# One software DMA queue shared by weight loads, gathers and result scatters: a new order, one more early weight and six output buffers

## Chip, core and metric

One core of one Trainium2 chip runs the whole program. Times are device microseconds. Each profile is of one of the executions whose times are listed. Chips differ (the kernel before had medians from 239.5 to 250.9 us in the five sets of rounds) and one core has slow executions too, so every comparison below is between kernels run on the same chip in the same rounds, or between stretches inside profiles. The record marks slow executions as such.

## The reference, cut to what matters

```
attn = masked_attention(q, k, v)          # 4 batches, 8 heads, 768 tokens, 64 dims
x    = attn as [3072 tokens, 512]
for e in range(8):                        # each token belongs to one of 8 experts
    out[tokens of e] = relu(x[tokens of e] @ w1[e]) @ w2[e]
# w1[e] is 512x1024, w2[e] is 1024x512, float32 in HBM
```

## The kernel before

Attention writes its result to a DRAM scratch tensor. Tokens are then gathered by expert, transposed, sent through two layers and scattered to their rows of the output. Three sorts of DMA are issued by GpSimd and share one software queue (q0 of the profile: 7936 packets, 26.75 MB): weight loads (float32 in HBM, cast to float16 on the way, 1 MiB landed), gathers of 128 token rows, and scatters of 128 result rows.

```
def load_w(e, which):                     # 16 of these, 4 buffers for each layer
    nc.gpsimd.dma_start(out=<fp16 tile>, in_=<fp32 weights in HBM>)

def load_xe(pr, g):                       # 28 gathers: 7 per pair of experts
    nc.gpsimd.indirect_dma_start(out=xe_of(pr, g), in_=x_d, in_offset=map_i[...])

def finish_group(pr, g, ps):              # 28 scatters: 7 per pair
    o = opool.tile(...)                   # one of 4 output buffers
    nc.vector.tensor_copy(out=o, in_=ps)  # the sums of TensorE's matmuls, 0.69 us
    nc.gpsimd.indirect_dma_start(out=out, out_offset=out_i[...], in_=o)

for pr in range(E // 2):                  # the late part of the expert stage
    layer2(a); layer2_half(pr); layer2(b_)        # 3 + 1 + 3 groups
    <weights for later experts>; <drain>; <gathers>
    for g in range(NG): x_transpose(pr + 2, g)    # TensorE, then a VectorE copy
    layer1(a + 4, 0, CAP); layer1(b_ + 4, 0, CAP)
# ... attention, early experts, routing and a fallback loop cut
```

The output copy and the copies of the transposes are both on VectorE, in program order. An output copy that waits for a buffer therefore holds back everything behind it (in the changed kernel the copy at 181.16 us had waited 6.10 us, and the transposes' copies followed at 181.76).

The softmax here doesn't subtract the row's maximum and nothing guards it: scores larger than these inputs give would overflow.

## Time and profile before

| | before |
|---|---|
| runs (the profile is of the second) | 239.22, 241.62, 238.91 us |
| span of the profile | 239.7 us |
| TensorE busy | 82% |
| start of expert 0's second layer to last matmul | 134.84 to 234.01, so 99.2 us |
| of it, TensorE standing still at two places | 12.09 and 3.48 us |

The fifth row is the one the change is about. The profile lines that show it stand in the prediction. In a timeline the columns are start, duration, engine, line, operation, operands, count, and in brackets the idle time before it with what ended it. The granted clock is the share of its full clock that TensorE was given, by the profile, and "halved" means 0.5 (in the kernel before from 149.1 to 162.7 us).

### The profile page before, as it was taken

The page shows a single profiled execution, that of the slowest core. Times are in us where ns is not written, and L with a number is a line of the kernel's source. Part 1 is how long each engine was busy: PE and PEld are TensorE (multiplying, and loading weights), DVE is VectorE, ACT ScalarE, POOL GpSimd, SP SyncE. Part 2 cuts the span into 40 slices and gives each one's busy share as a digit, 9 for nine tenths or more (in the row PEclk, how much of TensorE's full clock was granted, in tenths as well). Part 3 has the DMA queues.
Part 4 walks back from the last instruction along what each step waited for, and adds up shares of the span by engine and source line. Part 5 has one row for each costly group of instructions (what it writes and reads, how often), then busy time and mean ns, then how long its engine had stood idle before and what let it go on. Part 6 is the DMA issues. An engine that isn't in the chain of part 4 may idle for free. (4 is left out here: it accounts for less than half of the span.)

```text
span 239.7 us, 4769 instructions
## 1 busy us (share of the span) xinstructions
PE 197.7 (82%) x1935; PEld 123.7 (52%) x1935; DVE 107.8 (45%) x251; ACT 93.7 (39%) x117; POOL 110.3 (46%) x143
## 2 busy tenths in 40 slices
PE   0489999699998999988988992067999479999990
PEld 0235666456664666588988741035654145544440
DVE  1337899999968767642022130034003160033431
ACT  2177678548862787424655400001640005600000
POOL 0546675358153514743875460038611580036552
PEclk9999999999997999999999999559999999999998
DMA  6999999999999530699899899926999549913332
GB/s 209 300 314 288 307 288 244 299 340 291 242 320 328 128 131 26 122 280 243 163 198 263 151 215 214 252 108 122 213 215 228 210 178 176 182 45 133 136 117 89
DMA packets 42909, 49.79 MB, mean 208 GB/s; under 512 B 27263, under 2 KB 35712, under 8 KB 42882
## 3 DMA queue, kind: packets, MB, share of 16 engines
q0 software_dynamic: 7936, 26.75, 48.5%
q1 hardware_dynamic: 34368, 22.02, 32.9%
q10 hardware_dynamic: 578, 0.66, 1.1%
q8 instruction: 17, 0.28, 0.4%
q14 instruction: 10, 0.08, 0.1%
HBM read 56.76 MB, written 10.49 MB: 280 GB/s over the span
## 5 line engine op out<-in xcount | busy, mean ns | idle before, releaser
L333 ACT ACTIVATE eT<-sp 128x1024 f16<-128x1024 f32 (+2 forms) x68 | 60.3, 916 | 35.5 <-PE sp L311 34.7
L708 ACT ACTIVATE hT<-h 128x512 f16<-128x512 f32 (+2 forms) x48 | 32.1, 669 | 77.6 <-PE h L701 77.6
L732 PE MATMUL o<-w,hT 128*128 128x512 f16 x192 | 44.6, 389 | 15.6 <-DVE oute L714 15.6
L701 PE MATMUL h<-xT,w 128*128 128x256 f16 (+2 forms) x384 | 50.4, 290 | 1.6 <-DVE xT L686 1.6
L716 POOL DMA_INDIRECT out_dram<-oute,out_i x28 | 27.8, 994 | 51.6 <-DVE oute L714 30.1
L714 DVE COPY oute<-o 128x512 f32<-128x512 f32 x24 | 16.5, 692 | 74.9 <-PE o L732 54.6
L701 PEld LDWEIGHTS <-w 128*128 128x128 f16 x384 | 38.9, 114 | 12.1 <-DVE xT L686 1.7
L732 PEld LDWEIGHTS <-hT 128*128 128x128 f16 x192 | 18.7, 99 | 39.9 <-issue 19.5
L660 POOL DMA_INDIRECT xe<-x_tok,map_i x24 | 24.5, 1019 | 25.2 <-DVE xe L801 7.8
L387 PE MATMUL av<-ve,eT 128*128 128x65 f16 (+3 forms) x532 | 31.3, 196 | 4.9 <-DVE xb L400 2.8
L387 PEld LDWEIGHTS <-eT 128*128 128x128 f16 (+3 forms) x572 | 25.6, 99 | 15.3 <-issue 7.9
L311 PE MATMUL sp<-qT,kT 64*128 64x192 f16 (+6 forms) x244 | 26.0, 277 | 1.9 <-DVE kT L281 1.6
L311 PE MATMUL sp<-c16s 128*128 128x128 f16 (+1 forms) x132 | 25.9, 278 | 0.5 <-ACT eT L333 0.3
L155 POOL CAST q<-q 128x768 f16<-128x768 f32 x15 | 13.0, 869 | 23.6 <-PE tpq L276 11.8
L155 POOL CAST k<-k 128x768 f16<-128x768 f32 x16 | 13.2, 827 | 16.8 <-DMA k<-in_k_dram 15.8
L281 DVE COPY qT<-tpq 128x768 f16<-128x768 f16 x16 | 15.2, 950 | 8.2 <-PE tpq L276 8.2
L683 DVE COPY xT<-xtp 128x512 f16<-128x512 f16 x24 | 9.1, 418 | 21.1 <-PE xtp L676 20.4
L400 DVE TENSOR_TENSOR xb<-av,rcp 128x384 f16<-128x384 f32 x32 | 17.8, 557 | 1.1
L311 PEld LDWEIGHTS <-kT 64*128 64x128 f16 x244 | 9.7, 95 | 16.4 <-issue 7.1
L281 DVE COPY kT<-tpk 128x768 f16<-128x768 f16 x16 | 15.2, 948 | 3.2 <-PE tpk L276 3.2
L176 POOL CAST ve<-v 128x384 f16<-128x384 f32 x32 | 15.8, 524 | 0.8 <-DMA v<-in_v_dram 0.8
L276 PE MATMUL tpq<-c16s,q 128*128 128x128 f16 x96 | 9.4, 237 | 6.4 <-DVE q L155 5.4
(80 smaller groups left out, 130.2 us busy)
## 6 DMA issues: line engine op xcount, KB each, us to landing
w<-in_moe_w_dram POOLq DMA_DIRECT2D x16, 1024.0 KB, 11.6
q<-in_q_dram SPq DMA_DIRECT2D x16, 384.0 KB, 6.1
k<-in_k_dram SPq DMA_DIRECT2D x16, 384.0 KB, 6.1
v<-in_v_dram SPq DMA_DIRECT2D x32, 192.0 KB, 5.7
x_tok<-xb SPq DMA_DIRECT2D x4, 768.0 KB, 6.9
out_dram<-oute,out_i POOLq DMA_INDIRECT x28, 2.8
xe<-x_tok,map_i POOLq DMA_INDIRECT x24, 7.5
c16s<-c ACTq DMA_DIRECT2D x1, 336.5 KB, 4.6
```

The costliest lines, as they stand in the source:

```text
L155: eng.tensor_copy(out=t[:].rearrange("p t h d -> p h t d"), in_=q32_t[nm, n][:])
L281: nc.vector.tensor_copy(out=d[:], in_=cell["ps"][:].rearrange("d t p -> d p t"))
L311: nc.tensor.matmul(out=sp[:, c : c + w], lhsT=lhsT, rhs=rhs, start=bank not in begun, stop=True, skip_group_check=True,)
L333: nc.scalar.activation(out=eT[n, r // 3][:, r % 3, c0:c1], in_=sp[:, c0:c1], func=AF.Exp, scale=scale)
L387: nc.tensor.matmul(out=ps[m0:m1, it, :], lhsT=eT[n, r // 3][kk, r % 3, c : c + w], rhs=rhs, start=(x == 0), stop=(x == len(mms) - 1), skip ...
L400: nc.vector.tensor_tensor(out=xb[b][:, :, h * D : (h + 1) * D], in0=ps[:, :, 0:D], in1=rcp[:].unsqueeze(2).to_broadcast([P, NSO, D]), op=A ...
L660: nc.gpsimd.indirect_dma_start(out=xe_of(pr, g), out_offset=None, in_=x_d[0 : 1 + nb * S, :], in_offset=bass.IndirectOffsetOnAxis(ap=map_i ...
L701: nc.tensor.matmul(out=pv[:, a, c0:c1], lhsT=w_t[e, 1][:, c // 2, c % 2, fc * 512 + fr : (fc + 1) * 512 : 4], rhs=xT_t[e][:, c, c0:c1], st ...
L708: nc.scalar.activation(out=hT_t[e][:, 2 * f2 : 2 * f2 + 2, c0:c1], in_=pv[:, :, c0:c1], func=AF.Relu)
L714: nc.vector.tensor_copy(out=o[:], in_=ps[:])
L716: inst = nc.gpsimd.indirect_dma_start(out=out, out_offset=bass.IndirectOffsetOnAxis(ap=out_i[:, s : s + 1], axis=0), in_=o[:], in_offset=None,
L732: nc.tensor.matmul(out=ps[:], lhsT=hT_t[e][:, f, g * P : (g + 1) * P], rhs=w_t[e, 2][:, f // 4, f % 4, :], start=(f == 0), stop=(f == 7),)
```

## The change

The change spreads the weights between the scatters, so that fewer weights stand ahead of the results, starts one more weight during attention, and adds two output buffers. The arithmetic stays the same.

```diff
-    opool = ctx.enter_context(tc.tile_pool(name="moe_out", bufs=4))
+    opool = ctx.enter_context(tc.tile_pool(name="moe_out", bufs=6))
...
-        ws = {4: (0, 1), 8: (1, 1)}
+        ws = {4: (0, 1), 8: (1, 1), 11: (2, 1)}
...
-                load_w(2 + pr, 1)
+                load_w(*((3, 1), (0, 2))[pr])
...                                     # after attention: (0,2),(1,2) become (1,2),(2,2)
             if e < 2:
                 load_w(e + 4, 1)
-                load_w(e + 2, 2)
+    after = {
+        0: lambda: load_w(3, 2),
+        1: lambda: (load_w(6, 1), load_w(4, 2), load_w(7, 1), load_w(5, 2)),
+        2: lambda: load_w(6, 2),
+        3: lambda: (load_w(7, 2), nc.gpsimd.drain()),
+    }
     for pr in range(E // 2):
         layer2(a)
         layer2_half(pr)
+        if a in after: after[a]()
         layer2(b_)
-        <weights e+6 first layer, e+4 second layer, for both experts>
-        <drain if pr == 1>
-        <all 7 gathers of pair pr + 3>
+        if pr == 0: <gathers 0 to 2 of pair 3>
+        if b_ in after: after[b_]()
+        if pr == 0: <gathers 3 to 6 of pair 3>
```

More of the change, by code (lines that the diff above doesn't have):

```diff
@@ L837 @@
         load_xe(0, g)
-    load_w(0, 2)
+    load_w(1, 2)
     for g in (2, 5, 6):
         load_xe(1, g)
-    load_w(1, 2)
+    load_w(2, 2)
     for g in range(NG):
@@ L860 @@
         layer2_half(pr)
+        if a in after:
+            after[a]()
         layer2(b_)
-        for e in (a, b_):
-            if e + 6 < E:
-                load_w(e + 6, 1)
-            if e + 4 < E:
-                load_w(e + 4, 2)
-        if pr == 1:
-            nc.gpsimd.drain()
-        if pr + 3 < E // 2:
-            for g in range(NG):
-                load_xe(pr + 3, g)
+        if pr == 0:
+            for g in range(3):
+                load_xe(3, g)
+        if b_ in after:
+            after[b_]()
+        if pr == 0:
+            for g in range(3, NG):
+                load_xe(3, g)
         if pr + 2 < E // 2:
```

## The prediction

> **What bounds the kernel now.** I read the page's slices first, then TensorE's timeline in the expert stage, then the list of waits, then the software DMA queue. The chain of waits holds only the last 1.2 us, so it does not help. The slices:
>
> ```profile
> PE   0489999699998999988988992067999479999990
> ...
> PEclk9999999999997999999999999559999999999998
> DMA  6999999999999530699899899926999549913332
> ```
>
> TensorE is nearly full everywhere but slices 24 to 26 and 31: two holes, the first followed by a halved clock. DMA is busy in that first hole, so bytes are moving, but not the ones TensorE needs. The timeline of TensorE shows the edges:
>
> ```profile
> 141.96 3.63 PE L732 MATMUL o<-w,hT 128*128 128x512 f16 x16
> 157.68 3.57 PE L732 MATMUL o<-w,hT 128*128 128x512 f16 x8 [12.09 <-DVE oute L714]
> 161.05 1.06 PE L676 MATMUL xtp<-c16s,xe 128*128 128x128 f16 x8
> ...
> 184.41 3.63 PE L732 MATMUL o<-w,hT 128*128 128x512 f16 x16
> 191.53 1.89 PE L732 MATMUL o<-w,hT 128*128 128x512 f16 x8 [3.48 <-DVE oute L714]
> ```
>
> Both times the third token group of an expert's second layer waits for VectorE to copy results out of PSUM. It waited 12.09 us in the first hole (after expert 1) and 3.48 in the second (after expert 3). Why VectorE was late is in the list of waits from 90 us on:
>
> ```profile
> DVE oute L714 <- DMA out_dram<-oute,out_i: 20.3, 3, 14.1
> PE o L732 <- DVE oute L714: 15.6, 2, 12.1
> POOL xe L660 <- DMA w<-in_moe_w_dram: 5.0, 2, 4.7
> POOL xeh L660 <- DMA w<-in_moe_w_dram: 4.4, 1, 4.4
> ```
>
> VectorE had no free output buffer (four of them), because the scatters had not landed. The DMA view of 132 to 140 us and of 212 to 240 us gives the last thing needed, time from issue to landing:
>
> ```profile
> w<-in_moe_w_dram POOLq DMA_DIRECT2D x4, 1024.0 KB, 17.7
> out_dram<-oute,out_i POOLq DMA_INDIRECT x2, 18.5
> ...
> out_dram<-oute,out_i POOLq DMA_INDIRECT x14, 2.8
> ```
>
> A scatter takes 2.8 us in a quiet queue and 18.5 behind four weights. The tile view, one issue at a time: in block one the four weights are issued at 131.5 to 134.4; the second lands at 145.1 (132.2 + 12.9), the fourth at 156.1 (133.65 + 22.5), and the first three scatters, issued at 137.7, 139.5 and 141.2, land at 156.8, 157.5 and 158.1. In block two the weights issued from 163.2 land at 171.3, 177.3, 182.1, 187.1. So a weight lands about 8.2 us after the first issue, the next ones 5 to 6 us apart, and scatters come out strictly behind them, 0.65 us apart.
>
> The queue has a second limit. In block two the sixth gather is issued at 177.51, as the second weight lands, and the seventh at 182.90, as the third does: each is the DMA eight places later. I read this as at most eight software DMAs in flight.
>
> [...] halved from about 149.1, 3.5 us into the first hole, to 162.7. The 3.48 us hole did not trigger it.
>
> **The change part by part.**
>
> One: a third first-layer weight moves into attention (iteration 11), and the other early weights each move up one place, with the second-layer weight of expert 0 filling the last slot of iteration 14. GpSimd pays nothing new, only 0.77 us at about 72.8 instead of at 97.9. The cost is contention: beside the weight issued at 56.34, input loads took 10 to 11 us to land instead of about 6, and the next k cast waited 2.92 us. The loads still open at 73 are iteration 15's q, k and v, issued 72.8 to 77. They land about 81 now, so perhaps 86. Their casts run at 81.5 to 83.2, but TensorE first needs them at 92.2: some 9 us of slack against 5 of delay. I count zero. From 97.9 to 131.48 the queue holds as many weights and gathers in the same places, so the second layer of expert 0 starts at 134.84 as now.
>
> Two: block one shrinks from four weights to two before the scatters. The first lands at about 139.8, the second at 145.1, so the first four scatters at about 145.8, 146.5, 147.1, 147.7 instead of from 156.8. One weight is then placed after the fourth scatter (GpSimd at 144.1 + 1.0): it lands near 152.7, and the last three scatters of the pair by 154.7. The seventh copy needs the first buffer at 147.3, and it is free since 145.8. Hole one goes: 12.1 us. The cold clock goes with it: eight matmuls took 3.57 us against 1.89 after the second hole, and the stretch from the group's end to the first layer 4.14 (161.05 to 165.19) against 3.84 (193.25 to 197.09), so 1.9 to 2.0 us. Sum of the first hole: 14.0. As a check: with groups 1.78 us apart the third group would have started at 145.5, and the first layer of expert 4 at 151.2 instead of 165.2.
>
> Three: block two. GpSimd ends the last scatter issue at 149.1, issues three gathers of 1.31 us each, and the four weights from 153.1 (before: 163.2). The queue empties only at about 156, so landings are about 161.9, 167.2, 172.2 and 177.2, then four gathers to 178.9. TensorE, no longer held, starts the second layer of expert 2 at 151.2 + 12.1 = 163.3. Its first scatter is ready at 165.9, but sits behind two weights and four gathers and lands at about 179.6. Six buffers let six copies go; the seventh, ready at 175.9, waits for that landing until 179.7. The copies of the transposes stand behind it on VectorE. In the old second hole the first layer started 2.95 us after the end of the last such copy (194.14 to 197.09); so 179.7 + 0.69 + 2.95 = 183.3, against 175.9 + 3.84 = 179.7 unheld. A new hole costs 3.6 us where the old one cost 3.5: the weights come earlier, but TensorE arrives earlier by more.
>
> Four: the last two weights now go out one after the second half's fourth scatter and one at its end. They land by about 192; the drain behind them, which ended 2.4 us after the last landing before (212.3 against 209.9), ends near 195. The next scatter is ready only at 198. Nothing on the path.
>
> Sum: 14.0 + 3.5 - 3.6 = 13.9 us gained. TensorE's last matmul moves from 234.0 to about 220.1: 183.3 + 12.1 to the second layer of expert 4, and then the same 24.8 us that it takes now (209.22 to 234.01). The tail of 5.7 us stays, so the profile's span goes from 239.7 to about 225.8; the median from 239.22 to about 225.3. As the small chance of a cold clock is one-sided, I say 225.5.
>
> **Rivals.** First, the six buffers suffice: if the four weights of block two stream faster or start sooner by 3 us, the seventh copy is not held and the gain is 17.5, giving 222. For it: the weights queue at an almost empty ring; against it: 5 us spacing in both blocks. Second, the new hole trips the clock: [...] cold matmuls would add 2 us: 227.5. The 3.48 us hole that stayed warm speaks against it, its being longer now for it. Third, the extra weight in attention delays it: slice 12 already shows a dip of the clock (0.88 mean from 75 to 85), and k casts wait for DMA after both earlier weights. If the slack is misread, attention ends up to 3 us later: 228.5. Fourth, the scatters were held by the limit of eight in flight rather than by order; then six buffers and fewer weights ahead still relieve it, so the time is the same.
>
> **Range and chances.** 222 and 228.5 are the single rivals; a bit outside for two at once: 221.5 to 229.5. Faster by 2% needs below 234.4, which would take the loss of 9 of 13.9 us: faster 0.96, within 2% 0.03, slower 0.01.
>
> **What would show it.** The first hole: no wait of TensorE on an output copy after expert 1, the first scatter landing in about 8 us instead of 19, the first layer of expert 4 near 151, no half clock before it. The second: one wait of about 3.6 us on VectorE's seventh output copy of the pair near 176 to 180, released by a scatter's landing. The late loads: the k cast of iteration 15 a few us late, with TensorE's transposes near 92 unmoved. The prediction is wrong if the second layer of expert 0 starts later than 136, or if any new TensorE hole is over 5 us.

## The result, and the profile after

The median was 230.6 us (229.7 to 236.35, four runs) against 239.51 for the kernel before. The ratio of the fast runs was 0.9626, 95% interval 0.953 to 0.972. A ratio here is the mean time of one kernel's fast runs over that of the other's of the same rounds, so it isn't quite the ratio of the medians quoted (it takes in a fifth run of the changed kernel, 232.81 us). The change made the kernel clearly faster, but the time lies above the range of 221.5 to 229.5.

The same three rows of slices, after:

```profile
PE   1489999789998999989998899889997299999990
...
PEclk9999999976999999997999999999999859999996
DMA  6999999999999993289989989999999799022422
```

Of the two holes of TensorE one is left (slices 30 and 31, counted from 0), and the clock dips right after it. The timeline of TensorE from 90 us on:

```profile
134.93 5.34 PE L732 MATMUL o<-w,hT 128*128 128x512 f16 x24
...
151.47 12.27 PE L701 MATMUL h<-xT,w 128*128 128x448 f16 x64 [0.48 <-DVE xT L686]
163.57 5.34 PE L732 MATMUL o<-w,hT 128*128 128x512 f16 x24
...
175.89 0.61 PE L676 MATMUL xtp<-c16s,xe 128*128 128x128 f16 x8
182.23 2.11 PE L676 MATMUL xtp<-c16s,xe 128*128 128x128 f16 x16 [5.73 <-DVE xT L683]
184.43 0.58 PE L676 MATMUL xtp<-c16s,xeh 128*128 128x128 f16 x4
185.49 13.60 PE L701 MATMUL h<-xT,w 128*128 128x448 f16 x64 [0.47 <-DVE xT L686]
198.93 5.34 PE L732 MATMUL o<-w,hT 128*128 128x512 f16 x24
```

The first hole is gone: the first layer of expert 4 starts at 151.47 where it started at 165.19. The second hole is longer than it was, 5.73 us against 3.48. The work after it is slower too: the first layer of experts 6 and 7 takes 13.44 us (185.49 to 198.93), and the same work took 12.10 at 151.47. VectorE's timeline shows what the transposes waited for:

```profile
174.36 0.69 DVE L714 COPY oute<-o 128x512 f32<-128x512 f32 x1 [1.03 <-PE o L732]
181.16 0.69 DVE L714 COPY oute<-o 128x512 f32<-128x512 f32 x1 [6.10 <-DMA out_dram<-oute,out_i]
181.76 0.75 DVE L683 COPY xT<-xtp 128x512 f16<-128x512 f16 x2
```

The seventh output copy of the pair waits 6.10 us for a scatter to land, and the transposes' copies stand behind it. The DMA view gives the reason, for issues from 155 to 166 us and from 166 to 172 (the last column is the median time from issue to landing):

```profile
w<-in_moe_w_dram POOLq DMA_DIRECT2D x3, 1024.0 KB, 17.0
...
out_dram<-oute,out_i POOLq DMA_INDIRECT x2, 13.5
```

The scatters stand behind the second burst of weights and take 13.5 us in place of 2.8. Stage by stage:

| | before | after |
|---|---|---|
| second layer of expert 0 starts | 134.84 | 134.93 |
| first layer of expert 4 starts | 165.19 | 151.47 |
| first layer of expert 6 starts | 197.09 | 185.49 |
| first layers of 6 and 7 take | 12.13 | 13.44 |
| from there to the last matmul | 24.79 | 24.79 |
| stretch, expert 0's second layer to last matmul | 99.17 | 88.79 |
| span | 239.7 | 229.5 |

The last matmul came at 223.72; my own sum gives 179.7 + 0.69 + 2.95 + 12.13 + 24.79 = 220.26. So 3.46 us were missing, all of them between 175.9 and 198.9.

### The profile page after: what moved, and what is told of

The parts are those of the page before. It is cut to its first block, busy times and chain, and to the rows that moved or that the text cites.

```text
span 229.5 us, 4770 instructions
## 1 busy us (share of the span) xinstructions
PE 199.4 (87%) x1935; PEld 125.2 (55%) x1935; DVE 107.6 (47%) x251; ACT 93.7 (41%) x117; POOL 110.1 (48%) x143
## 5 line engine op out<-in xcount | busy, mean ns | idle before, releaser
L701 PE MATMUL h<-xT,w 128*128 128x256 f16 (+2 forms) x384 | 53.0, 299 | 1.7 <-DVE xT L686 1.7
L701 PEld LDWEIGHTS <-w 128*128 128x128 f16 x384 | 39.7, 115 | 14.1 <-issue 2.9
L732 PE MATMUL o<-w,hT 128*128 128x512 f16 x192 | 42.6, 379 | 0.0
L387 PE MATMUL av<-ve,eT 128*128 128x65 f16 (+3 forms) x532 | 32.0, 198 | 4.0 <-DVE xb L400 2.7
L387 PEld LDWEIGHTS <-eT 128*128 128x128 f16 (+3 forms) x572 | 26.2, 101 | 14.4 <-issue 7.6
L155 POOL CAST q<-q 128x768 f16<-128x768 f32 x15 | 12.4, 829 | 28.1 <-DMA q<-in_q_dram 15.4
L676 PE MATMUL xtp<-c16s,xe 128*128 128x128 f16 x96 | 8.8, 240 | 7.9 <-DVE xT L683 7.8
## 6 DMA issues: line engine op xcount, KB each, us to landing
w<-in_moe_w_dram POOLq DMA_DIRECT2D x16, 1024.0 KB, 11.2
```

The lines of the kernel that those rows point to most:

```text
L155: eng.tensor_copy(out=t[:].rearrange("p t h d -> p h t d"), in_=q32_t[nm, n][:])
L387: nc.tensor.matmul(out=ps[m0:m1, it, :], lhsT=eT[n, r // 3][kk, r % 3, c : c + w], rhs=rhs, start=(x == 0), stop=(x == len(mms) - 1), skip ...
L701: nc.tensor.matmul(out=pv[:, a, c0:c1], lhsT=w_t[e, 1][:, c // 2, c % 2, fc * 512 + fr : (fc + 1) * 512 : 4], rhs=xT_t[e][:, c, c0:c1], st ...
L732: nc.tensor.matmul(out=ps[:], lhsT=hT_t[e][:, f, g * P : (g + 1) * P], rhs=w_t[e, 2][:, f // 4, f % 4, :], start=(f == 0), stop=(f == 7),)
```

## The experiments

The theory: the software queue is first in, first out (before, the fourth weight landed at 156.2 and the scatters behind it from 156.8 on). A scatter that stands behind weights lands late, 19.1 us after its issue behind four of them, and when the buffers run out VectorE stops (14.1 us in the kernel before), and TensorE with it (12.09 us). If the stop is long enough the clock halves as well, as it did in that hole and not in the one of 3.48 us. The rivals were that the order or the buffers alone do everything, that the hole is the wait for gathers behind the weights, and that the slow work after the hole comes from DMA traffic and not from the clock.

"Stretch" below is always from the start of expert 0's second layer to the end of the last matmul, in the profile. It leaves out attention, whose end differs between runs by several us.

| run | ratio to before | stretch | first layers of 4 and 5, of 6 and 7 |
|---|---|---|---|
| before | 1 | 99.17 | 12.10, 12.13 |
| changed | 0.9626 | 88.79 | 12.10, 13.44 |
| 1 changed again | 0.962 | 89.58 | 12.11, 14.46 |
| 2 six buffers alone | 0.9725 | 94.06 | 14.58, 12.13 |
| 3 order alone | 0.976 | 91.49 | 12.11, 12.10 |
| 4 filler, 20 matmuls | 0.9458 | 88.87 | 12.11, 13.30 |
| 5 seven buffers | none | 83.55 | 12.10, 13.51 |
| 6 early weight alone | none | 96.03 | 12.10, 13.81 |
| 7 early weight undone | none | 90.93 | 12.11, 13.73 |
| 8 burst taken apart | none | 86.93 | 12.76, 12.11 |
| 9 changed again | 0.9474 | 88.19 | 12.11, 14.18 |
| 10 gathers first | 0.9708 | 91.88 | 13.71, 14.12 |
| 11 gathers first, seven buffers | 0.9275 | 81.49 | 12.11, 12.10 |
| 12 burst apart, no drain | 0.9365 | 85.07 | 13.19, 13.79 |
| 13 filler, 27 matmuls | 0.9518 | 88.04 | 13.74, 12.10 |
| 14 changed again | 0.9535 | 89.99 | 12.11, 14.11 |
| 15 as run 11 | 0.9257 | 81.49 | 12.11, 12.11 |

Runs 1 to 4 shared a chip, as did 5 to 8, 9 to 12, and 13 to 15. On the chip of 5 to 8 only two of seven runs of the kernel before were fast (246.09 and 246.37), so no ratio was given; those four are read by their stretches. All outputs were correct. A stretch is that of one profile.

A view of the granted clock is quoted for the kernels before and after and for runs 4, 12, 13 and 14. In the views that have both, the time of a first layer (64 matmuls) times its mean clock is 12.0 to 12.1 us (12.10 at 1.00 and 13.44 at 0.90 in the changed kernel, 13.79 at 0.88 in run 12, 14.11 at 0.85 in run 14). For the other runs I read a first layer well over 12.1 us as one at a partly halved clock; that is a reading, not a view.

### Run 1: the changed kernel again

> The changed kernel once more, unaltered, as the yardstick for this chip. Theory (first in, first out, plus the clock): about 0.96 of the kernel before, the second hole of TensorE again near 5.7 us and again followed by a halved clock. If the halved clock after the second hole was chance, this profile shows the second stretch of first-layer work at 12.1 us instead of 13.4.

Median 232.4 us against 241.95. The hole was 5.79 us, and the first layer after it took 14.46 (13.44 in the first profile, where the clock was halved for 6.8 us from 181.4). In all four profiles of the changed kernel this stage took 13.4 to 14.5 us: the halved clock there is no chance.

### Run 2: six buffers, old order

```diff
- name="moe_out", bufs=4     (kernel before)
+ name="moe_out", bufs=6
```

> The kernel before with six output buffers and nothing else. Queue-order theory: the first scatter still lands near 157, so the seventh output copy waits for it, TensorE's first hole shrinks from 12.1 to about 9 us, but the second burst of weights is issued near 158.5 instead of 163.2 and the second hole vanishes; in all some 6 us less than before, ratio about 0.973. Rival (the order of the ring is the gain and the buffers only follow it): under 2 us less, ratio above 0.99.

Nearly as the queue theory has it: median 235.56 against 241.95. TensorE's first wait and the second pair's transposes were

```profile
157.44 2.11 PE L676 MATMUL xtp<-c16s,xe 128*128 128x128 f16 x16 [10.21 <-DVE xT L683]
...
188.88 0.71 PE L676 MATMUL xtp<-c16s,xe 128*128 128x128 f16 x8 [0.67 <-DMA out_dram<-oute,out_i]
```

The first hole is still 10.21 us (about 9 expected), because the seventh copy still waits for the first scatter behind four weights; the second is gone. Buffers alone are worth 5.1 us of the stretch (99.17 to 94.06). I had not foreseen that the first layer after the hole would be slow, 14.58 us in place of 12.10.

### Run 3: new order, four buffers

```diff
- name="moe_out", bufs=6     (changed kernel)
+ name="moe_out", bufs=4
```

> The changed kernel with four output buffers, so the new order alone. Queue-order theory: the first hole is about 2 us, the second about 7 us, because the fifth copy of that pair now waits for the scatter that lands near 182; time about 4 us above the changed kernel, ratio to before about 0.98. Rival (buffers carry nothing once the ring is in order): ratio the same as the changed kernel's, 0.96.

Median 234.83. TensorE's timeline:

```profile
146.44 1.89 PE L732 MATMUL o<-w,hT 128*128 128x512 f16 x8 [0.85 <-DVE oute L714]
...
182.08 3.57 PE L732 MATMUL o<-w,hT 128*128 128x512 f16 x8 [7.13 <-DVE oute L714]
185.45 1.06 PE L676 MATMUL xtp<-c16s,xe 128*128 128x128 f16 x8
```

The first hole shrinks to 0.85 us by order alone (about 2 expected), but the second grows to 7.13: the order moved the wait into the second burst. The stretch is 7.7 us shorter than before, so order and buffers aren't additive (5.1 and 7.7 alone, about 10 together). By the ratios, 0.9725 and 0.976 with overlapping intervals, it can't be said which of the two alone is worth more.

### Runs 5, 10, 11: which wait makes the second hole

Run 5 gives the changed kernel a seventh buffer, run 10 moves the last four gathers ahead of the four weights, run 11 does both.

```diff
  runs 10 and 11 (changed kernel)
-            for g in range(3): load_xe(3, g)
+            for g in range(NG): load_xe(3, g)
         if b_ in after: after[b_]()
-        if pr == 0:
-            for g in range(3, NG): load_xe(3, g)
  runs 5 and 11
- name="moe_out", bufs=6
+ name="moe_out", bufs=7
```

> The changed kernel with seven output buffers, so that the seventh output copy of a pair no longer waits for the first scatter. Theory: TensorE's second hole shrinks to the wait for the last four gathers, which stand behind the four weights and land near 179.5 to 180.5: some 2 us instead of 5.7, no halved clock after it, and 4 to 5 us less than the changed kernel (ratio to before about 0.943). Rival (the hole is set by the gathers alone and the buffer wait only hides it): less than 1 us gained.

Median 235.0 us on the slow chip; the stretch fell to 83.55, 4.6 to 6.4 us below the four profiles of the changed kernel. No transpose wait was over 0.81 us, and that one was for a gather, as expected:

```profile
190.13 0.75 PE L676 MATMUL xtp<-c16s,xe 128*128 128x128 f16 x8 [0.81 <-DMA xe<-x_tok,map_i]
```

The expected whole clock did not come in this profile: the first layer still took 13.51 us. I had the hole right and its effect on the clock wrong. The profile is of a slow execution (238.35 us); whether the clock halved there in the fast ones is not shown.

> The changed kernel with the last four gathers moved ahead of the four weights, six buffers. Queue-order theory: the weights start 5 us later, so the first scatter of experts 2 and 3 lands 4 to 5 us later, the seventh copy waits for it and TensorE's second hole grows from 5.7 to 9 or 10 us; 3 to 5 us above the changed kernel, although TensorE's own inputs, the gathers, come earlier. Rival (the hole is the wait for gathers behind weights): the hole vanishes and the time falls by some 5 us.

This is the run with the opposite sign: TensorE's own inputs come earlier and the kernel is slower, 234.31 us against 229.6 for the changed kernel beside it (run 9). VectorE's seventh copy and TensorE after it:

```profile
181.93 0.69 DVE L714 COPY oute<-o 128x512 f32<-128x512 f32 x1 [7.20 <-DMA out_dram<-oute,out_i]
183.01 2.11 PE L676 MATMUL xtp<-c16s,xe 128*128 128x128 f16 x16 [6.83 <-DVE xT L683]
```

The hole grew to 6.83 us, less than the 9 to 10 expected, since here the first layer of experts 4 and 5 itself ran 1.6 us longer (13.71, against 12.11 in run 9) and TensorE came later to the wait. Counted from the start of the stretch, the hole ended 3.6 us later than in run 9 (49.72 against 46.16). The hole is the buffer's wait. The gathers alone do not explain it.

> The same with seven output buffers: now neither the gathers nor a buffer hold TensorE at the second hole. Theory: no hole over 1 us in the expert stage, no halved clock there; the stretch from the second layer of expert 0 to the last matmul is 81.7 to 83 us against 89 for the changed kernel; about 6 to 7 us less, ratio to before about 0.935. Rival (the scatters that pile up behind the drain cost it back): the stretch stays above 85.

Median 226.66 us, ratio 0.9275 against 0.9474 for run 9. With both waits gone the second pair's transposes run through, and the first layer takes 12.10:

```profile
179.69 0.61 PE L676 MATMUL xtp<-c16s,xe 128*128 128x128 f16 x8
180.96 0.71 PE L676 MATMUL xtp<-c16s,xe 128*128 128x128 f16 x8 [0.67 <-DVE xT L683]
181.86 0.71 PE L676 MATMUL xtp<-c16s,xe 128*128 128x128 f16 x8 [0.19 <-DVE xT L683]
182.76 0.38 PE L676 MATMUL xtp<-c16s,xeh 128*128 128x128 f16 x4 [0.18 <-DVE xT L683]
183.62 12.27 PE L701 MATMUL h<-xT,w 128*128 128x448 f16 x64 [0.47 <-DVE xT L686]
```

The stretch of 81.49 us is the work alone: four second-layer blocks (one for each pair), two first-layer blocks and their transposes without a stop. So the changed kernel's 88.2 to 90.0 held 6.7 to 8.5 us of hole and halved clock together.

Run 9 was the yardstick:

> The changed kernel unaltered once more, as the yardstick for the three runs beside it, since chips differ in when attention ends. From the start of expert 0's second layer to TensorE's last matmul it should take 88.8 to 89.5 us as in the two earlier profiles; about 0.962 of before.

Median 229.6 against 242.17, stretch 88.19, hole 4.88, first layer 14.18. The ratio was 0.947 where 0.962 had been seen twice; on the chip of run 14 it was 0.9535. Their intervals overlap, so this need not be the chips, but I compare ratios within a chip only.

### Runs 6 and 7: the early weight

```diff
  run 6 (kernel before): the weight of expert 2 in iteration 11 and not in 14
- ws = {4: (0, 1), 8: (1, 1)}
+ ws = {4: (0, 1), 8: (1, 1), 11: (2, 1)}
- load_w(2 + pr, 1)
+ if pr == 0: load_w(3, 1)
  run 7 (changed kernel): the reverse; each later weight one place on
- 0: lambda: load_w(3, 2),
+ 0: lambda: (load_w(2, 2), load_w(3, 2)),
```

> The kernel before with only the one first-layer weight moved into attention (iteration 11), nothing else. Theory: the load is hidden and nothing later changes: ratio 1.00. Rival (the extra load delays attention by up to 3 us): the second layer of expert 0 starts later than 136 and the ratio is above 1.005.

Mean of its fast runs 246.0 us, of the kernel before 246.2, but from two fast runs only. This excludes a large cost or gain, not half a per cent. The rival's other sign did appear: expert 0's second layer started at 142.20, later than 136. On this chip it started late without the early weight too (run 7, 141.50), and the kernel before has no profile there, so the sign decides nothing.

> The changed kernel with that one weight back in iteration 14 and every following weight one place later, so that two weights and not one stand after the fourth scatter. Theory: the second burst begins 5 us later, the first scatter of experts 2 and 3 lands near 186.5 instead of 181, and the time is 5 to 6 us above the changed kernel, ratio to before about 0.985. Rival (the early weight brings nothing by itself): the same as the changed kernel, 0.962.

Its fast runs had a mean of 241.9 us, 0.982 of those two. The seventh copy waited 8.24 us in place of 5.3 to 6.4 in the changed kernel's profiles, and the stretch was 90.93. The direction is as expected and the size is not: the wait grew by 2 to 3 us, not 5. In this profile attention ended 6.6 us later than in the changed kernel's first one, and when the two later weights went out at 150.70 the queue had nearly run dry (DMA share 0.07 from 150 to 151), so that it had less to catch up on. That this is the reason is argued, not shown. On that chip it had no yardstick, so I leave the size open.

### Runs 8 and 12: the second burst taken apart, and the drain

```diff
  run 8 (changed kernel with all gathers first, six buffers)
-  1: (w1 of 6, w2 of 4, w1 of 7, w2 of 5)      2: (w2 of 6)   3: (w2 of 7, drain)
+  1: (w1 of 6, w1 of 7)   2: (w2 of 4, w2 of 5)   3: (w2 of 6, w2 of 7, drain)
  run 12: as run 8, without the drain
```

> The changed kernel with the second burst taken apart: all seven gathers first, then only the two first-layer weights of experts 6 and 7; the second-layer weights of 4 and 5 after the half group's scatter, those of 6 and 7 at the pair's end. Six buffers as in the changed kernel. Theory: the first scatter of experts 2 and 3 lands near 174, before the seventh copy needs its buffer at 176, so the second hole is gone altogether and the clock stays whole: TensorE ends 6 to 7 us earlier than in the changed kernel, less about 1 us because the drain now ends near 202 and holds the scatters; ratio to before about 0.938. Rival (something else than the scatter's place in the queue makes the hole): the hole stays above 3 us.

The hole went without another buffer, as the queue theory says: the transposes at 186 waited at most 0.67 us. (The 12.76 us of its first layer of 4 and 5 hold a pause of 0.48 us; the matmuls around it took 0.19 us each, as in a first layer of 12.1.) But the last pairs took 29.6 us in place of 24.8. GpSimd's timeline:

```profile
188.46 1.53 POOL L187 DMA_DIRECT2D w<-in_moe_w_dram  x2
213.06 1.07 POOL L716 DMA_INDIRECT out_dram<-oute,out_i  x1 [23.06 <-issue]
214.44 1.03 POOL L716 DMA_INDIRECT out_dram<-oute,out_i  x1 [0.30 <-issue]
```

The drain held GpSimd for 23 us, while output copies waited for buffers again. That was more than the 1 us I had allowed.

> The earlier run with the second burst taken apart (gathers first, then only the first-layer weights of 6 and 7), now without the drain instruction on GpSimd after the last weight. There the drain held GpSimd for 23 us and the last fourteen scatters piled up behind it, so the last pair lost 4.8 us. Theory: without it the scatters go out as their copies come, the last two pairs take 24.8 us and the whole stretch 82 to 83 us, ratio about 0.935. Rival (the drain is not what holds the scatters, the queue is): the last two pairs stay near 29 us; or what the drain did is paid at the end of the kernel: the tail after the last matmul grows from 5.8 us.

Both halves of this were right at once. Without the drain the last two pairs took 24.8 us again (193.63 to 218.41), and the tail after the last matmul grew from 5.8 to 9.0 us: part of what the drain does is paid at the end. Median 228.63, ratio 0.9365. The stretch was 85.07, not 82 to 83, because both first-layer stages were slow, 13.19 and 13.79 us (the second at a mean clock of 0.88), here with no hole ahead of them: the longest wait of the transposes before them was 1.28 and 0.67 us. This profile is of a slow execution (229.2 us). Its mean granted clock, 0.963, makes by my estimate 17 us at half speed in all; the two fast ones, with 0.983 and 0.982, had about 8, so their stretch may well have been the expected one.

### Runs 4 and 13: the clock by itself

The changed kernel with idle matmuls placed in the second hole; they write a score tile that nobody reads, so the results stay right.

```diff
             for g in range(NG):
+                if pr == 1 and g == 2:
+                    <20 (run 4) or 27 (run 13) matmuls 128*128 128x512 into spare PSUM tiles>
                 x_transpose(pr + 2, g)
```

> The changed kernel with twenty idle 512-column matmuls (into a score tile that nobody reads) placed where TensorE stands still in the second hole, 4.3 us at full clock. Clock theory: the hole's length stays (it is set by the scatter's landing), but the clock stays whole, so the following transposes and first layer take 2 us less: the span falls by about 2 us against the unaltered one where that one goes cold. Rival (the slow first layer after the hole comes from DMA traffic or weight loads and not from the clock): first-layer stretch stays at 13.4 us and the time does not fall.

Median 228.8 against 232.4 for run 1, but the stretch was 88.87 and the clock still halved, for 3.4 us from 182.8. The filler took 4.48 us and ended at 179.1, the transposes began at 180.98, and 1.9 us of standing still was followed by sparse small transposes. The experiment had failed to make its own condition, so its faster time proves nothing about the clock.

> The changed kernel with twenty-seven idle 512-column matmuls in the second hole, 5.8 us, so that TensorE works until the moment the transposes are released (the earlier try with twenty ended 1.9 us too soon [...]). Clock theory: no halved clock from 175 to 200; from the end of the seventh output copy to the second layer of expert 4 about 15.1 us instead of 17.1 to 18.1, so 2 to 3 us less than the changed kernel beside it, the hole itself unchanged. Rival (the slow first layer after the hole comes from the DMA traffic): that stretch stays at 17 us or more.

Run 14 beside it was the unaltered kernel:

> The changed kernel unaltered, yardstick of the other two on this chip: ratio to before 0.945 to 0.965, a hole of 5 to 6 us near 176 to 182 and a halved clock after it.

The two windows views, of the hole and of the first layer of experts 6 and 7; columns are stretch, length, busy time of PE, PEld, DVE, ACT and POOL, then the granted clock, the DMA share and GB/s. Run 14, unaltered:

```profile
174.80:180.85 6.05, 0.00 (x1) 0.00 (x1) 1.08 (x3) 0.00 (x0) 2.21 (x3) 0.76 0.61 222
184.10:198.21 14.11, 14.11 (x64) 7.63 (x65) 0.06 (x1) 6.42 (x7) 0.71 (x1) 0.85 0.75 168
```

Run 13, with the hole filled:

```profile
178.00:183.80 5.80, 5.80 (x30) 2.71 (x29) 1.35 (x3) 0.00 (x0) 3.79 (x4) 1.00 0.64 170
186.21:198.31 12.10, 12.10 (x64) 7.24 (x64) 0.14 (x1) 6.42 (x7) 0.00 (x0) 1.00 0.77 175
```

The same 64 matmuls beside the same DMA share (0.77 and 0.75) take 12.10 us at a whole clock and 14.11 at 0.85, both in fast executions: the slow first layer is the clock, not the traffic. The total hardly moved (229.29 and 230.18 us, ratios 0.9518 and 0.9535 with overlapping intervals), where I had expected 2 to 3 us. In this profile TensorE came later to the wait, since the first layer of 4 and 5 took 13.74 us at a partly halved clock (0.51 from 151.2 to 154.6). So the scatter landed earlier relative to TensorE, and the filler ran 2.4 us past the end of the seventh copy (181.40 to 183.80); it gave back what it won. Filling a hole isn't a remedy; removing it is.

### Run 15: the better version

> Seven buffers with all gathers ahead of the four weights, a second time, as the candidate that beats both kernels: no hole over 1 us in the expert stage, stretch from expert 0's second layer to the last matmul 81.5 to 83 us, 2 to 3.5% less than the changed kernel beside it. Rival (the gain seen on the other chip was that chip's): less than 1% below the changed kernel.

Median 223.68 us, ratio 0.9257 against 0.9535 for run 14 on the same chip: 2.9% below the changed kernel (0.9257 / 0.9535), 7.4% below the kernel before. The stretch is 81.49 us, to the hundredth that of run 11. Both these profiles are of slow executions (228.47 and 227.67 us), in which attention ended late, at 139.0 and 138.2; no wait of TensorE's transposes is over 0.67 us in either.

## Why the prediction was wrong, point by point

The direction was right, and so was the cause of each hole; the price of the second hole was not: 7.1 us in place of 3.6. The forecast was 225.5 and the measured median 230.6. Of the two signs that the prediction had named as proof against it, one came: a new hole of over 5 us (5.73).

**Part one, the early weight hidden in attention: right in the profile.** The casts of iteration 15 came later, as the loads did, and TensorE's transposes of that iteration did not. GpSimd, after:

```profile
85.28 0.83 POOL L155 CAST q<-q 128x768 f16<-128x768 f32 x1 [5.67 <-DMA q<-in_q_dram]
86.38 0.83 POOL L155 CAST k<-k 128x768 f16<-128x768 f32 x1 [0.27 <-DMA k<-in_k_dram]
```

The k cast ran at 82.39 before; the transposes of k ran at 91.69, and at 92.51 before. Expert 0's second layer began at 134.93 against a predicted 134.84.

**Part two, the first hole goes, with its cold clock, 14.0 us: right.** The first layer of expert 4 was predicted for 151.2 and came at 151.47. But the margin was luck. The second weight landed at 146.7, not 145.1, and the seventh copy, with 1.5 us to spare in the prediction, started at 147.74, some 0.3 us later than the pace of the copies before it (1.72 us apart, the sixth at 145.72). The scatters behind two weights took 7.3 and 8.4 us (issued 141.28 and 139.56). Runs 2 and 3 add what the sum could not: order and buffers each remove a large part alone.

**Part three, "A new hole costs 3.6 us where the old one cost 3.5": this step failed.** Its cause was named correctly, its size wasn't. Against the unheld case (175.9 + 3.84 = 179.7) the first layer of expert 6 started 5.8 us late, and then ran 1.3 us longer, 7.1 us in all. The missing 3.46 us of the sum consist of three terms:

- *The landing of the scatter, 1.5 us.* The copy was predicted to be released at 179.7 and was at 181.16. I let "the queue" empty "only at about 156", but the weight placed between the scatters landed at 155.3 (144.13 + 11.2), not 152.7 (1.6 us of this it had from the weight before it), and the scatters and gathers behind it kept the queue full to about 158.4. All later landings moved: the first weight of the burst 163.4 for 161.9, the last 179.0 for 177.2.
- *The transposes after the hole, 0.7 us.* From the end of the seventh copy to the first layer it took 3.64 us (181.85 to 185.49), not 2.95.
- *The first layer, 1.3 us.* 13.44 for 12.13. Run 13 shows that this is the clock, and this trace agrees: the clock was halved until 188.2, so the first layer ran 2.7 us at half speed, which costs some 1.4 us. The second term falls in the same halved stretch; that it is the clock too is argued, not separately shown.

The last two terms are the second rival, which I priced rightly at 2 us but called a "small chance" and left out of the sum. All four profiles of the changed kernel have it; in the other three the first layer alone lost 2.0 to 2.4 us. I had reasoned from one hole of 3.48 us that had left the clock whole (1.00 from 177.29 to 197.09). The changed kernel's holes were 4.88 to 6.06 us long, and after each the first layer was slow; what decides after which hole the clock halves, the runs do not show.

**Part four, the late weights, 0: right.** The last weight landed at 197.9 and the drain ended at 200.4 (182.4 + 17.98), later than my 195; the next scatter was ready at 201.8. Nothing waited, but with 1.4 us to spare where I had counted 3. Run 8 shows what a little more would have cost.

**From the span to the median.** The rest of the gap is in this conversion. I carried over that the median of before was 0.5 us under its profile's span (239.22 and 239.7). That profile was of a run of 241.62 us, the slowest of three. In both profiles a run's time is 1.8 to 1.9 us above its own span (241.62 and 239.7, 231.32 and 229.5), and the new kernel's median is 1.1 us above the span (230.6 and 229.5). So 1.6 us of the 5.1 us were an artefact of a slow profiled run, and 3.5 were the second hole; the span itself was 229.5 for a predicted 225.8.

**The rivals.** The first, that six buffers suffice, was wrong: the seventh copy was held. The second happened. The third, a delay of attention, did not show in the profile. The fourth, the limit of eight in flight as the true holder, was not needed to explain the second hole: the first scatter of experts 2 and 3 was issued at 166.48, at once after its copy, and still took 14.6 us to land. The limit exists beside it (the last point of the closing list says what it is); it held the second weight of the burst to 155.90, just after the landing at 155.3.

## What to carry to other kernels

In this queue the transfers landed in the order of their issue (in the kernel before, the scatters at 156.8 to 158.1, right behind the weight at 156.2), so a small store that frees a buffer must be counted with every large load issued ahead of it; a burst needs enough buffers for all the results that come while it drains, or it must be split. When a wait is removed, the engine arrives earlier at the next one: rework that one with the new arrival times, and add the clock's recovery to a hole of some 5 us as a part of its price, not as a chance (here the eight matmuls after the holes of 3.18 and 3.48 us took the full-speed 1.89 us; after every one from 4.88 to 12.09 us, in ten profiles, TensorE was slow: 3.57 us for such eight or 13.4 to 14.6 for the first layer in place of 12.1; run 13 shows that the clock can halve without a hole too). Before a span is turned into a forecast of a median, look whether the profiled run was a typical one.

## What else the traces show

- The clock can halve without a hole. In run 13, in a fast execution, its mean was 1.00 from 147.8 to 151.2 us and 0.51 from 151.2 to 154.6, and from 135.06 to there TensorE had no wait over 0.67 us. Run 10, fast too, had a first layer of 13.71 us in place of 12.1 after waits of at most 0.67. In run 8, a slow execution, sixteen matmuls after a hole of only 2.26 us took 5.30 us in place of 3.63. What set it off in these was not shown.
- The median of the last 14 scatters, in a quiet queue, was 2.8 us from issue to landing in the kernel before. With weights ahead it was 14.6 us behind the second burst (changed kernel) and 19.1 behind four (before).
- The loads cast on the way. 1 MiB landed from 2 MiB read took 4.8 to 6.0 us each in the queue (landings 171.3, 177.3, 182.1, 187.1 before).
- The drain on GpSimd lasted until 2.4 to 2.5 us after the last software DMA had landed (212.3 for 209.9 before, 200.4 for 197.9 after), and without it (run 12) the kernel's tail was 9.0 us in place of 5.8.
- At most eight software DMAs were in flight (a gather was issued at 177.51 as the DMA eight places ahead landed at 177.3). The packed trace of the kernel before shows where it comes from: the software DMAs signal on eight semaphores in turn, and each gather from 166.47 to 182.90 waits for the one that it is to raise itself. So it is the program's; whether the chip has a limit too, these runs do not tell.
